# Score and softmax tiles turned over in 32x32 blocks by VectorE instead of by TensorE, in an attention-plus-feed-forward kernel with a hand-listed order

## The chip, the cores and the metric

The kernel runs on one NeuronCore of one Trainium2 chip. The metric is the device time of one execution in microseconds (us). Five engines work beside each other, each through its own queue in order: TensorE (PE in the rows, with its weight loads as PEld), VectorE (DVE), ScalarE (ACT), GpSimd (POOL) and SyncE (SP), which issues all the DMA transfers of this kernel.

## The reference

Two stages, all in fp32. First attention between 512 tokens and 32 state rows, per batch (8) and head (8, of width 64), in both directions; then a feed-forward layer with a rational activation over the 8 x (512 + 32) = 4352 rows that come out.

```python
scores = scale * x @ state.T                     # 512 x 32 per head
scores = scores - scores.max(-1)                 # over the 32 state rows
a = exp(scores); a /= a.sum(-1) + 1e-09
xread = a @ state
scores2 = scale * state @ x.T                    # 32 x 512 per head
scores2 = scores2 - scores2.max(-1)              # over the 512 tokens
a2 = exp(scores2); a2 /= a2.sum(-1) + 1e-09
sread = a2 @ x
x = concat([xread, sread])                       # rows x 512 columns
h = x @ w_in                                     # 512 -> 2048
P = a0 + a1*h + a2*h**2 + a3*h**3
Q = 1 + |b0|*|h| + |b1|*h**2
out = (P / (Q + 1e-6)) @ w_out                   # 2048 -> 512
```

## The kernel before, in words

**Work units.** The feed-forward is cut into 72 units: nine groups of eight. Group b below 8 is the 512 tokens of batch b, the ninth group holds all state rows. A unit n takes 256 of the 2048 hidden columns (u = n mod 8). The list name `F:n:i` is its first product (six matmuls of 128 x 512 for each of two column halves), `FC` and `FB` read the product h on ScalarE, `mu`, `po`, `qd`, `g1`, `g2`, `g3` are six VectorE instructions of 128 x 1024, `qa`, `ln`, `ex` three on ScalarE, and `gl` is one on GpSimd. `mh:n:t` and `ml:n:t` are the second product for token tile t (four and two matmuls of 128 x 512), which read the high and the low part of g (`gh`, `gl`). Products are taken with operands split in a rounded high part and a low rest, which is why one product of the reference is three here.

**Attention of a batch.** `scores` puts 32 x 256 products in PSUM so that a head pair's state row stands in a quadrant of 32 partitions and tokens run along the free axis. `sc_copy` (ScalarE, L414) copies them to SBUF as `sT`. The direction over tokens takes its maximum and its exponential from `sT` (`col_max`, `col_exp`). For the direction over the 32 state rows, `row_T` turns `sT` over: eight products of 128 x 128 with the identity (L434) into the PSUM tile `ps_s`; `row_max` (L458) and `row_sub` (L466) on VectorE read it, and `row_sub` writes the SBUF tile `e1`. Then `row_exp` (ScalarE), `row_sum`, `row_eps` (VectorE) and `row_norm` (GpSimd) follow, all on `e1`. `a_T` turns `e1` back with eight products (L434) into the PSUM tile `ps_a`; `a_hi` (ScalarE, L517) and `a_lo` (VectorE, L521) write its high and low part to `aT`, which the batch's eight `F` units read. `e2_T` is a third set of eight products. In the trace `e1` and `e2` are both called e.

**Weights.** The weights come as 64-bit floats in 32 pieces of 512 KB (`lr`). `cp` (ScalarE, L299), `jr` (VectorE, L309, two instructions per pair of pieces) and `jl` (VectorE, L325) make fp32 of them. For `w_out`, `sp` splits them (ScalarE L336, GpSimd L337). For `w_in`, `X` multiplies the state into the weights on TensorE (L606), `XA` copies the result out (ScalarE L618), `XS` stores it to DRAM, and `lm` and `fs` fetch it later for the units (L646, L647).

**Order.** `ORDER` is a list of 2266 such tokens. The program is emitted in that order, so the order of each engine's queue is the list's; the framework adds the waits. PSUM has two buffers of 128 x 1024 (tag h), shared by the units' h, `X`, and for batches 1 to 7 the tiles of `scores`, `row_T`, `e2_T`, `a_T` and `sread`. Four more banks hold the four running output tiles.

Of the kernel before, what the change touches and what calls it, by code (L numbers as in the profile page):

```python
# [18 lines left out]
P = 128  # L19
# [4 lines left out]
    "warm:8 lt:0:0 lr:0 cp:0 ls:0:2 scores:0:0 lr:1 jr:0 cp:1 jl:0 lc cb lt:0:1 scores:0:1 sc_copy:0:0 "  # L24
    "col_max:0:0 sc_copy:0:1 col_max:0:1 col_scale:0:0 lr:2 cp:2 X:0 fh:0 XA:0 col_scale:0:1 "
    "col_exp:0:1 lr:3 row_T:0:1 row_max:0:1 ls:2:8 row_sub:0:1 jw:0 XS:0 jr:1 X:3 fo:0 row_T:0:0 "
    "col_exp:0:0 X:1 row_exp:0:1 row_sum:0:1 lr:4 row_max:0:0 lr:5 XA:3 XS:3 cp:3 XA:1 row_sub:0:0 XS:1 "
    "e2_T:0:0 e2_copy:0:0 X:2 row_exp:0:0 lr:6 row_eps:0:1 row_norv:0:1 jl:1 a_T:0:1 row_sum:0:0 "
    "row_eps:0:0 a_hi:0:1 cp:4 XA:2 XS:2 e2_T:0:1 lr:7 X:5 row_norv:0:0 e2_copy:0:1 a_T:0:0 a_lo:0:1 "
    "col_eps:0 a_hi:0:0 a_lo:0:0 XA:5 XS:5 X:4 fh:1 cp:6 F:0:1 lq:0:0 fo:1 F:0:0 cp:5 jr:2 jl:2 b0a "  # L30
    "jr:3 XA:4 FC:0 lq:0:1 FB:0 qd:0 F:1:1 cp:7 F:1:0 lr:9 FB:1 FC:1 jl:3 XS:4 sp:7 sp:6 mu:0 po:0 qa:0 "
    "ln:0 qd:1 ex:0 jw:1 X:9 XA:9 lr:8 cp:8 lr:11 mu:1 po:1 lr:10 cp:10 XS:9 sread:0:0 cp:9 X:8 XA:8 "
    "XS:8 col_norm:0 jr:5 jr:4 jl:4 X:6 fh:2 fo:2 sread:0:1 sr_copy:0 g1:0 g2:0 XA:6 cp:11 lr:13 XS:6 "
    "qa:1 lr:15 sr_T:0 sr_fin:0 lr:14 jl:5 lr:12 g3:0 gl:0 X:12 fh:3 XA:12 XS:12 F:2:1 F:2:0 FC:2 FB:2 "
    "fo:3 sp:10 mh:0:0 mu:2 X:13 XA:13 XS:13 ln:1 sp:11 cp:12 qd:2 ex:1 mh:0:1 ml:0:1 cp:14 mh:0:2 "
    "ml:0:2 po:2 g1:1 g2:1 X:7 XA:7 jr:6 X:10 XA:10 ml:0:0 jr:7 cp:15 jl:7 lt:1:1 g3:1 gl:1 cp:13 qa:2 "
    "ln:2 X:11 XS:7 F:3:1 F:3:0 FB:3 FC:3 XA:11 jl:6 mh:0:3 ml:0:3 mh:1:3 ex:2 lt:1:0 scores:1:0 "
    "scores:1:1 XS:10 mu:3 qd:3 po:3 sp:14 sp:15 ml:1:3 lr:16 sc_copy:1 cp:16 lr:17 jw:4 mh:1:0 "
    "col_max:1 qa:3 lr:21 XS:11 X:17 X:14 XA:17 jw:2 jr:8 ml:1:0 g1:2 g2:2 g3:2 cp:17 ml:1:2 "
    "col_scale:1 XA:14 lr:20 X:15 XS:17 mh:1:2 row_T:1 row_max:1 row_sub:1 ln:3 mh:2:1 XS:14 jl:8 jw:3 "  # L40
    "cp:20 XA:15 XS:15 col_exp:1:0 cp:21 X:16 XA:16 lr:18 col_exp:1:1 gl:2 XS:16 lr:19 col_eps:1 fh:4 "
    "fo:4 X:18 XA:18 XS:18 row_exp:1 mh:1:1 cp:18 jr:10 jl:10 ml:1:1 X:20 fh:5 XA:20 fo:5 cp:19 F:4:1 "
    "F:4:0 FB:4 jr:9 col_norm:1 jl:9 X:21 FC:4 mh:2:2 mu:4 qd:4 sp:18 mh:2:3 XA:21 ml:2:1 sp:19 mh:2:0 "
    "lr:25 ex:3 ml:2:3 po:4 lr:22 XS:20 cp:22 g1:3 lr:23 cp:23 lr:24 cp:24 jr:12 XS:21 X:19 XA:19 XS:19 "
    "X:23 XA:23 cp:25 jr:11 jl:11 qa:4 lr:26 g2:3 g3:3 ml:2:0 sp:23 jl:12 X:22 sp:22 F:5:1 F:5:0 XS:23 "
    "FB:5 FC:5 mh:3:0 ml:2:2 mu:5 po:5 XA:22 cp:26 qd:5 lr:27 ln:4 mh:3:2 mh:3:1 XS:22 X:24 ex:4 g1:4 "
    "XA:24 XS:24 fh:6 fo:6 lm:8 mh:3:3 gl:3 lq:1:1 qa:5 ml:3:3 ml:3:0 X:26 XA:26 XS:26 ml:3:2 g2:4 g3:4 "
    "e2_T:1 e2_copy:1 row_sum:1 jr:13 cp:27 gl:4 X:25 XA:25 X:28 row_eps:1 row_norm:1:1 XS:25 jl:13 "
    "jw:7 mh:4:0 ln:5 ex:5 fh:7 F:6:1 XA:28 fo:7 g1:5 row_norm:1:0 F:6:0 FC:6 FB:6 qd:6 fs:8 ml:4:0 "
    "sp:26 ml:4:3 sp:27 XS:28 X:27 XA:27 lr:30 cp:30 ml:3:1 mu:6 po:6 qa:6 ln:6 ml:4:1 mh:4:2 lq:1:0 "  # L50
    "mh:4:3 X:30 XA:30 sread:1:0 sread:1:1 sr_copy:1 lr:28 g2:5 g3:5 gl:5 ex:6 mh:5:1 lr:31 mh:4:1 "
    "sr_T:1 sr_fin:1 cp:31 XS:27 XS:30 lr:29 X:29 XA:29 X:31 XA:31 mh:5:0 a_T:1 F:7:0 jr:15 F:7:1 jl:15 "
    "cp:28 ml:5:2 sp:31 mh:5:2 ml:5:3 g1:6 g2:6 a_hi:1 ml:4:2 a_lo:1 F:8:0 F:8:1 ml:5:1 sp:30 jr:14 "
    "cp:29 ml:5:0 FC:7 FB:7 mh:5:3 jl:14 qd:7 sp:29 sp:28 mh:6:3 mh:6:2 mu:7 po:7 mh:6:0 mh:6:1 lm:9 "
    "fs:9 FB:8 qd:8 qa:7 g3:6 F:9:1 F:9:0 gl:6 ml:6:2 ml:6:3 ln:7 ex:7 g1:7 mh:7:1 mh:7:2 FC:8 mu:8 "
    "po:8 FC:9 lm:10 ml:6:1 fs:10 FB:9 mh:7:3 F:10:1 g2:7 qa:8 ln:8 ex:8 F:10:0 g3:7 gl:7 ml:7:0 lm:11 "
    "ml:7:2 ml:7:1 qd:9 qa:9 ml:6:0 mu:9 po:9 FC:10 lm:13 lt:2:0 g1:8 FB:10 g2:8 g3:8 lt:2:1 scores:2:0 "
    "scores:2:1 mh:7:0 fl:7:2 gl:8 mu:10 po:10 qd:10 sc_copy:2 col_max:2 lq:2:1 ml:7:3 fl:7:3 mh:8:2 "
    "fl:7:1 fs:11 mh:8:3 mh:8:1 ml:8:1 ln:9 ml:8:3 ex:9 row_T:2 F:11:0 g1:9 g2:9 fl:7:0 mh:8:0 ml:8:0 "
# [872 lines left out]
```

## Time and profile before

| | us |
|---|---|
| median of 3 runs | 691.34 (690.94 to 692.08) |
| the profiled execution | 690.54 |
| its span, first to last instruction | 688.7 |
| TensorE busy | 661.9 (96%) |
| VectorE busy | 620.1 (90%) |
| ScalarE busy | 524.1 (76%) |
| GpSimd busy | 298.7 (43%) |
| mean granted TensorE clock | 0.987 of full speed |

The device time is 1.84 us longer than the span. Busy shares are means over the whole program; the program has a stage in which weights are fetched and converted, about 100 us long, a long middle in which one batch's units follow on another's, and an end of some 7 us.

### The profile page before, as it was taken

The page shows a single profiled execution, that of the slowest core. Times are in us where ns is not written, and L with a number is a line of the kernel's source. Part 1 is how long each engine was busy: PE and PEld are TensorE (multiplying, and loading weights), DVE is VectorE, ACT ScalarE, POOL GpSimd, SP SyncE. Part 2 cuts the span into 40 slices and gives each one's busy share as a digit, 9 for nine tenths or more (in the row PEclk, how much of TensorE's full clock was granted, in tenths as well). Part 3 has the DMA queues.
Part 4 walks back from the last instruction along what each step waited for, and adds up shares of the span by engine and source line. Part 5 has one row for each costly group of instructions (what it writes and reads, how often), then busy time and mean ns, then how long its engine had stood idle before and what let it go on. Part 6 is the DMA issues. An engine that isn't in the chain of part 4 may idle for free.

```text
span 688.7 us, 11564 instructions
## 1 busy us (share of the span) xinstructions
PE 661.9 (96%) x4602; PEld 525.3 (76%) x4602; DVE 620.1 (90%) x589; ACT 524.1 (76%) x641; POOL 298.7 (43%) x172
## 2 busy tenths in 40 slices
PE   6688889999999999999999999999999999999997
PEld 4455556778887778878887888788878788888895
DVE  4788689999999999999999999999899889998996
ACT  5889789887876876877778677777887777666773
POOL 0024146554554454434554444354444445445542
PEclk8989999999999999999999999999999999999999
DMA  7988877605122300451015022221203021300311
GB/s 290 327 298 327 304 290 277 225 37 196 64 77 92 127 17 25 125 190 39 18 60 199 15 98 72 92 82 71 78 33 137 2 75 55 99 0 33 107 47 30
DMA packets 29434, 81.49 MB, mean 118 GB/s; under 512 B 3268, under 2 KB 3396, under 8 KB 29380
## 3 DMA queue, kind: packets, MB, share of 16 engines
q1 hardware_dynamic: 29380, 80.75, 33.8%
q8 instruction: 36, 0.59, 0.4%
q14 instruction: 18, 0.15, 0.1%
HBM read 52.95 MB, written 27.79 MB: 117 GB/s over the span
## 4 chain that ended last, share of the span: by engine, by line
PE 77%; DVE 7%; DMA 6%; ACT 5%; issue 2%; POOL 1%; SPq 0%; POOLq 0%; ACTq 0%; DVEq 0%
PE h L687 25%; DMA m_dram<-xo 3%; DMA raw<-in_w_in_dram 2%; ACT xo L618 2%; PE o__3063 L760 2%; PE ps_x L606 2%; PE o__5992 L760 2%; PE o__3659 L760 2%; PE o__4266 L760 2%; PE o__3652 L760 2%; PE o__3604 L760 2%; PE o__5977 L760 2%; PE o__5430 L760 2%; PE o__3107 L760 2%; PE o__4244 L760 2%
## 5 line engine op out<-in xcount | busy, mean ns | idle before, releaser
L750 POOL TENSOR_TENSOR gl<-C,L 128x1024 fp32r<-128x1024 f32 (+1 forms) x71 | 168.9, 2379 | 271.1 <-DVE C L743 170.0
L687 PE MATMUL h<-aT,m 128*128 128x512 f32 x768 | 188.6, 392 | 0.8 <-ACT xo L618 0.8
L687 PEld LDWEIGHTS h<-aT,m 128*128 128x128 f32 x768 | 143.1, 188 | 33.1 <-ACT xo L618 2.9
L699 ACT ACTIVATE C<-h,cst 128x1024 f32<-128x1024 f32 (+1 forms) x72 | 83.1, 1156 | 40.9 <-PE h L687 33.3
L706 ACT ACTIVATE A<-h,cst 128x1024 f32<-128x1024 f32 (+1 forms) x72 | 76.9, 1068 | 47.1 <-PE h L687 41.7
L731 DVE SCALAR_TENSOR_TENSOR gh<-C,cst,L 128x1024 fp32r<-128x1024 f32 (+1 forms) x72 | 95.6, 1328 | 13.1 <-ACT L L802 9.5
L720 DVE SCALAR_TENSOR_TENSOR A<-A,b0a,h 128x1024 f32<-128x1024 f32 (+1 forms) x72 | 87.4, 1214 | 14.2 <-ACT A L706 10.4
L647 POOL TENSOR_TENSOR m<-m_sb,m 128x512 fp32r<-128x512 f32 x56 | 75.0, 1348 | 46.1 <-ACT m L646 22.0
L743 DVE SCALAR_TENSOR_TENSOR C<-C,cst,A 128x1024 f32<-128x1024 f32 (+1 forms) x72 | 91.0, 1263 | 2.1
L714 DVE SCALAR_TENSOR_TENSOR C<-C,cst,h 128x1024 f32<-128x1024 f32 (+1 forms) x72 | 87.7, 1219 | 1.9
L737 DVE SCALAR_TENSOR_TENSOR A<-A,gh 128x1024 f32<-128x1024 f32 (+1 forms) x72 | 87.5, 1216 | 1.7
L710 DVE TENSOR_TENSOR C<-C,h 128x1024 f32<-128x1024 f32 (+1 forms) x72 | 83.0, 1154 | 5.3 <-ACT C L699 2.7
L726 ACT ACTIVATE A<-A 128x1024 f32<-128x1024 f32 (+1 forms) x72 | 72.7, 1012 | 15.4 <-DVE A L720 15.4
L792 ACT ACTIVATE L<-A 128x1024 f32<-128x1024 f32 (+1 forms) x72 | 73.0, 1015 | 3.4 <-POOL gl L750 0.5
L802 ACT ACTIVATE L<-L 128x1024 f32<-128x1024 f32 (+1 forms) x72 | 73.1, 1015 | 1.8
L606 PE MATMUL ps_x<-win_sb,st 64*32 64x256 f32 x1024 | 39.6, 432 | 12.3 <-ACT xo L618 6.1
L337 POOL TENSOR_TENSOR wo<-cv_r,wo 128x512 fp32r<-128x512 f32 x16 | 23.3, 1476 | 59.8 <-ACT wo L336 59.6
L606 PEld LDWEIGHTS ps_x<-win_sb,st 64*32 64x32 f32 x1024 | 18.5, 116 | 28.1 <-issue 10.8
L646 ACT CAST m<-m_sb 128x512 fp32r<-128x512 f32 x56 | 33.9, 615 | 2.9 <-PE h L687 2.9
L618 ACT COPY xo<-ps_x 128x1024 f32<-128x1024 f32 (+1 forms) x32 | 28.8, 908 | 5.3 <-DMA m_dram<-xo 4.1
L299 ACT ACTIVATE cv_y<-raw 128x512 f32<-128x512 f32 x32 | 21.9, 695 | 11.1 <-DMA raw<-in_w_in_dram 8.7
L687 PEld LDWEIGHTS h<-sh,m 128*128 128x128 f32 x192 | 24.1, 191 | 0.6
(266 smaller groups left out, 1124.0 us busy)
## 6 DMA issues: line engine op xcount, KB each, us to landing
m_sb<-m_dram SPq DMA_DIRECT2D x56, 256.0 KB, 3.7
m_dram<-xo SPq DMA_DIRECT2D x24, 512.0 KB, 4.6
out_dram<-o_sb SPq DMA_DIRECT2D x34, 256.0 KB, 3.3
xT_sb<-in_xT_dram SPq DMA_DIRECT2D x16, 512.0 KB, 5.0
raw<-in_w_in_dram SPq DMA_DIRECT2D x16, 512.0 KB, 6.8
raw<-in_w_out_dram SPq DMA_DIRECT2D x16, 512.0 KB, 6.0
x_sb<-in_x_dram SPq DMA_DIRECT2D x16, 512.0 KB, 5.0
w_in_dram<-win_sb SPq DMA_DIRECT2D x8, 512.0 KB, 4.2
```

The lines of the kernel that those rows point to most:

```text
L647: nc.gpsimd.tensor_tensor(m[:, 1], t, m[:, 0].bitcast(F32), op=ALU.subtract)
L687: nc.tensor.matmul(h[:, ci * W : (ci + 1) * W], l, r, start=(q == 0), stop=(q == len(seq) - 1),)
L699: nc.scalar.activation(e["C"], e["h"], AF.Identity, scale=cst[:, 3:4], bias=cst[:, 2:3])
L706: nc.scalar.activation(e["A"], e["h"], AF.Abs, scale=cst[:, 5:6])
L710: nc.vector.tensor_tensor(e["C"], e["C"], e["h"], op=ALU.mult)
L714: nc.vector.scalar_tensor_tensor(e["C"], e["C"], cst[:, 1:2], e["h"], op0=ALU.add, op1=ALU.mult)
L720: nc.vector.scalar_tensor_tensor(e["A"], e["A"], b0a, e["h"], op0=ALU.add, op1=ALU.mult)
L731: nc.vector.scalar_tensor_tensor(e["gh"], e["C"], cst[:, 0:1], e["L"], op0=ALU.add, op1=ALU.mult)
L737: nc.vector.scalar_tensor_tensor(e["A"], e["A"], 1.0 + 1e-6, e["gh"].bitcast(F32), op0=ALU.add, op1=ALU.mult)
L743: nc.vector.scalar_tensor_tensor(e["C"], e["C"], cst[:, 0:1], e["A"], op0=ALU.add, op1=ALU.subtract)
L750: eng.tensor_tensor(e["gl"], e["C"], e["L"], op=ALU.mult)
L760: nc.tensor.matmul(O[t], e[l][:, j * W + t * P : j * W + (t + 1) * P], wo[:, k, 2 * u + j, :], start=(place == FIRST[n // U, t] and i + j ...
```

## The change

`row_T` and `a_T` become VectorE block transposes: one instruction that turns every 32 x 32 block over in its own place. Heads stand in quadrants of 32 partitions with 32 state rows each, so a block of tokens by state rows is such a block. `row_T` reads the PSUM tile of `scores` directly and writes `e1` in SBUF; `ps_s` and `ps_a` are gone. `row_max` and the subtraction now read `e1`. The subtraction is on GpSimd for all but the first half of batch 0 (`row_sup`). `a_T` writes a new SBUF tile `eT`, which for batches 1 to 7 has the buffer of `e2`; `a_hi` and `a_lo` read that, and `a_lo` is on GpSimd for batches 2, 3 and half of batch 0 (`a_lp`), on VectorE for the rest.

The list is ordered anew from its first token to its last, with 2266 tokens again. Beside the above it has other engines for some steps: 9 of the 32 copies `XA` are on VectorE (`XV`, four of 128 x 512 and five of 128 x 1024); 15 of the 16 pairs of `jr` are on GpSimd (`jp`); 3 of the 16 splits `sp` have their second half on VectorE (`sv`); one more `gl` and one more copy of an output tile are on VectorE (`gv`, `fv`). At the start SP issues the two halves of batch 0's `xT` and the first state rows before any weights. In the code:

```diff
@@ ORDER, first line @@
-    "warm:8 lt:0:0 lr:0 cp:0 ls:0:2 scores:0:0 lr:1 jr:0 cp:1 jl:0 lc cb lt:0:1 scores:0:1 sc_copy:0:0 "
+    "warm:8 lt:0:1 ls:0:2 lt:0:0 scores:0:0 scores:0:1 row_T:0:0 row_max:0:0 row_sub:0:0 lr:0 cp:0 "
...
@@ -329,12 +329,12 @@
     def store_win(u):
         nc.sync.dma_start(w_in32[u], win_t[u])
 
-    def conv_split(i):
+    def conv_split(i, eng):
         _, u, k = unit(i)
         m = CV[i // 2][1][:, k].bitcast(F32)
         f = 2 * u + k
         nc.scalar.copy(wo[:, 0, f, :], m)
-        nc.gpsimd.tensor_tensor(
+        eng.tensor_tensor(
             wo[:, 1, f, :], m, wo[:, 0, f, :].bitcast(F32), op=ALU.subtract
         )
 
@@ -365,6 +365,9 @@
                 for j in range(2)
             ]
         return ps_h.tile([P, 2, S], F32, name=name, tag="h")
+
+    def flat(t):
+        return t.rearrange("p j t -> p (j t)") if len(t.shape) == 3 else t
 
     def half(t, j):
         if isinstance(t, list):
@@ -438,7 +441,9 @@
                 )
 
     def row_T(b, j=None):
-        transposes(b, "ps_s", 2, TS[b]["sT"], j)
+        e1 = once(b, "e1", at_tile("e1", [P, 2, S]))
+        for i in (0, 1) if b == 0 and j is None else (j,):
+            nc.vector.transpose(flat(half(e1, i)), flat(half(TS[b]["ps"], i)))
 
     def col_exp(b, j):
         T = TS[b]
@@ -456,16 +461,16 @@
     def row_max(b, j=None):
         mx = once(b, "mx", at_tile("mx", [P, NT * 8], 2))
         nc.vector.tensor_reduce(
-            stat(mx, j), slots(TS[b]["ps_s"], j), axis=AX.X, op=ALU.max
-        )
-
-    def row_sub(b, j=None):
+            stat(mx, j), slots(TS[b]["e1"], j), axis=AX.X, op=ALU.max
+        )
+
+    def row_sub(b, j=None, eng=None):
         T = TS[b]
-        e1 = once(b, "e1", at_tile("e1", [P, 2, S]))
+        e1 = slots(T["e1"], j)
         mx = stat(T["mx"], j)
-        nc.vector.tensor_tensor(
-            slots(e1, j),
-            slots(T["ps_s"], j),
+        (eng or nc.vector).tensor_tensor(
+            e1,
+            e1,
             mx.unsqueeze(2).broadcast_to([P, mx.shape[1], NS]),
             op=ALU.subtract,
         )
@@ -509,18 +514,19 @@
         )
 
     def a_T(b, j=None):
-        transposes(b, "ps_a", 2, TS[b]["e1"], j)
-
-    def a_hi(b, j=None):
+        t = once(b, "eT", lambda: at.tile([P, 2, S], F32, name="eT", tag="e2" if b else "e2T"))
+        nc.vector.transpose(flat(half(t, j)), flat(half(TS[b]["e1"], j)))
+
+    def a_hi(b, j=None, copy=None):
         if b not in AT:
             AT[b] = at.tile([P, 2, 2, S], F32R, name="aT", tag="aT", bufs=2)
-        nc.scalar.copy(half(AT[b][:, 0], j), half(TS[b]["ps_a"], j))
-
-    def a_lo(b, j=None):
+        (copy or nc.scalar.copy)(half(AT[b][:, 0], j), half(TS[b]["eT"], j))
+
+    def a_lo(b, j=None, eng=None):
         a = AT[b]
-        nc.vector.tensor_tensor(
+        (eng or nc.vector).tensor_tensor(
             half(a[:, 1], j),
-            half(TS[b]["ps_a"], j),
+            half(TS[b]["eT"], j),
             half(a[:, 0].bitcast(F32), j),
             op=ALU.subtract,
         )
@@ -821,7 +827,8 @@
         "jr": lambda k: join_rest(k, nc.vector),
         "jp": lambda k: join_rest(k, nc.gpsimd),
         "jl": join_low,
-        "sp": conv_split,
+        "sp": lambda i: conv_split(i, nc.gpsimd),
+        "sv": lambda i: conv_split(i, nc.vector),
         "fh": fold_hi0,
         "fo": fold_lo0,
         "fs": fold_split,
@@ -861,6 +868,8 @@
         "fd": store,
         "lc": load_const,
         "cb": spread_const,
+        "a_lp": lambda b, j=None: a_lo(b, j, nc.gpsimd),
+        "row_sup": lambda b, j=None: row_sub(b, j, nc.gpsimd),
         "row_norv": lambda b, j: row_norm(b, j, nc.vector),
         "b0a": lambda: nc.scalar.activation(b0a, cst[:, 4:5], AF.Abs),
     }
```

TensorE's queue around the scores of batch 5 (`ps_s` is the transposed scores, `o` the running output tiles, `h` a unit's first product). Before:

```order
L760 MATMUL o__3659<-wo,gl 128x512 x2
L760 MATMUL o__3604<-wo,gl 128x512 x2
L434 MATMUL ps_s<-ident,sT 128x128 x8
L760 MATMUL o__3652<-wo,gh 128x512 x4
L687 MATMUL h<-aT,m 128x512 x18
L760 MATMUL o__3604<-wo,gl 128x512 x4
```

and now, from the batch's scores (`ps_sc`) on:

```order
L407 MATMUL ps_sc<-xT_sb,st 32x256 x16
L766 MATMUL o__3559<-wo,gl 128x512 x2
L766 MATMUL o__3564<-wo,gh 128x512 x4
L766 MATMUL o__3607<-wo,gh 128x512 x4
L766 MATMUL o__3607<-wo,gl 128x512 x2
L766 MATMUL o__3616<-wo,gh 128x512 x4
```

The eight products into `ps_s` have gone out of the queue, and nothing stands in their place but the second products that were around them.

VectorE's queue at the same place (`mx` is the row maximum, `cm` the column maximum, `e_3739` and `e_3667` are e1 of batch 5). Before:

```order
L418 TENSOR_REDUCE cm<-sT 128x2
L720 SCALAR_TENSOR_TENSOR A<-A,b0a,h 128x1024
L428 TENSOR_SCALAR cm<-cm 128x2
L743 SCALAR_TENSOR_TENSOR C<-C,cst,A 128x1024
L458 TENSOR_REDUCE mx<-ps_s 128x32
L466 TENSOR_TENSOR e_3739<-ps_s,mx 128x1024
L731 SCALAR_TENSOR_TENSOR gh<-C,cst,L 128x1024
```

and now:

```order
L421 TENSOR_REDUCE cm<-sT 128x2
L726 SCALAR_TENSOR_TENSOR A<-A,b0a,h 128x1024
L737 SCALAR_TENSOR_TENSOR gh<-C,cst,L 128x1024
L743 SCALAR_TENSOR_TENSOR A<-A,gh 128x1024
L431 TENSOR_SCALAR cm<-cm 128x2
L749 SCALAR_TENSOR_TENSOR C<-C,cst,A 128x1024
L446 STREAM_TRANSPOSE e_3667<-ps_sc 128x1024
L463 TENSOR_REDUCE mx<-e_3667 128x32
L737 SCALAR_TENSOR_TENSOR gh<-C,cst,L 128x1024
```

The transpose has come in ahead of the row maximum, and the subtraction behind it has left for GpSimd's queue; a second transpose (`eT`) stands 25 instructions further on.

GpSimd's queue at the start of the program (`wo` the low part of `w_out`, `cv_r` the joined weight bits). Before, from its first piece of work on:

```order
L337 TENSOR_TENSOR wo<-cv_r,wo 128x512 x2
L750 TENSOR_TENSOR gl<-C,L 128x1024
L337 TENSOR_TENSOR wo<-cv_r,wo 128x512 x2
L750 TENSOR_TENSOR gl<-C,L 128x1024
L337 TENSOR_TENSOR wo<-cv_r,wo 128x512 x2
```

and now:

```order
L309 TENSOR_SCALAR cv_r<-raw 128x512 x4
L512 TENSOR_TENSOR e_127<-e_127,rs 128x512
L471 TENSOR_TENSOR e_127<-e_127,mx 128x512
L309 TENSOR_SCALAR cv_r<-raw 128x512 x2
L527 TENSOR_TENSOR aT<-eT,aT 128x512
L309 TENSOR_SCALAR cv_r<-raw 128x512 x2
L337 TENSOR_TENSOR wo<-cv_r,wo 128x512 x2
L309 TENSOR_SCALAR cv_r<-raw 128x512 x4
L756 TENSOR_TENSOR gl<-C,L 128x1024
```

Joins of weight bits and batch 0's softmax steps now stand ahead of the first split and the first `gl`.

## Rows read from the trace of the kernel before

**Rows 1.** The page's span, and the busy time of each engine (us, share of the span, instructions).

```profile
span 688.7 us, 11564 instructions
PE 661.9 (96%) x4602; PEld 525.3 (76%) x4602; DVE 620.1 (90%) x589; ACT 524.1 (76%) x641; POOL 298.7 (43%) x172
```

**Rows 2.** Busy time of each engine in five stretches of the span: from and to in us, length, then busy us and instructions of PE, PEld, DVE, ACT and POOL, the granted TensorE clock, the share of the DMA engines and GB/s.

```profile
0.00:100.00 100.00, 79.73 (x1091) 50.41 (x1092) 73.57 (x99) 77.81 (x113) 20.12 (x18) 0.91 0.84 305
100.00:140.00 40.00, 39.75 (x456) 28.38 (x455) 38.56 (x35) 36.69 (x48) 25.50 (x15) 1.00 0.72 258
140.00:620.00 480.00, 478.16 (x2688) 390.16 (x2687) 450.96 (x389) 366.63 (x422) 223.08 (x122) 1.00 0.23 77
620.00:682.00 62.00, 62.00 (x365) 55.13 (x365) 55.73 (x68) 42.38 (x59) 30.00 (x18) 1.00 0.16 52
682.00:688.70 6.70, 2.25 (x9) 1.22 (x7) 1.27 (x2) 0.59 (x1) 0.00 (x0) 0.96 0.26 78
```

**Rows 3.** Waits of TensorE from 100 us on: who waited for whom, us in total, times, longest.

```profile
PE o__4923 L760 <- POOL gl L750: 1.0, 1, 1.0
PE o__2418 L760 <- POOL gl L750: 0.5, 1, 0.5
PE o__1819 L760 <- POOL gl L750: 0.4, 1, 0.4
PE ps_sr L539 <- DVE C L714: 0.2, 1, 0.2
```

**Rows 4.** The two sets of products with the identity that the change touches, batches 1 to 7 (duration ns min/median/max, first and last start in us), and the timeline of TensorE around one set, batch 7's (start us, us, what).

```profile
L434 PE MATMUL ps_s<-ident,sT x56: 270/272/273, 72.6 to 510.4; 128*128 128x128 f32 x56
L434 PE MATMUL ps_a<-ident,e x56: 270/272/273, 127.3 to 549.7; 128*128 128x128 f32 x56
...
509.62 1.04 PE L434 MATMUL ps_s<-ident,sT 128*128 128x128 f32 x8
510.42 1.17 PE L760 MATMUL o__4244<-wo,gh 128*128 128x512 f32 x4
```

**Rows 5.** Groups of VectorE instructions from 100 to 682 us (busy us, mean ns of one | idle before).

```profile
L521 DVE TENSOR_TENSOR aT<-ps_a,aT 128x1024 fp32r<-128x1024 f32 x7 | 8.5, 1217 | 1.4 <-ACT aT L517 1.4
...
L466 DVE TENSOR_TENSOR e<-ps_s,mx 128x1024 f32<-128x1024 f32 x6 | 7.3, 1224 | 0.2
L458 DVE TENSOR_REDUCE mx<-ps_s 128x32 f32<-128x1024 f32 x6 | 7.3, 1217 | 1.0 <-PE ps_s L434 1.0
...
L657 DVE TENSOR_TENSOR m<-win_sb,m 128x512 fp32r<-128x512 f32 x8 | 7.1, 903 | 0.3 <-issue 0.2
...
L309 DVE TENSOR_SCALAR cv_r<-raw 128x512 int32<-128x512 uint32 x6 | 5.8, 1014 | 0.0
...
L750 DVE TENSOR_TENSOR gl<-C,L 128x512 fp32r<-128x512 f32 x1 | 0.7, 693 | 0.1
```

**Rows 6.** Groups of GpSimd instructions from 100 to 682 us, same columns.

```profile
L750 POOL TENSOR_TENSOR gl<-C,L 128x1024 fp32r<-128x1024 f32 x61 | 151.8, 2489 | 227.4 <-DVE C L743 135.2 <-PE h L687 20.2 <-ACT m L646 10.5
L647 POOL TENSOR_TENSOR m<-m_sb,m 128x512 fp32r<-128x512 f32 x56 | 75.0, 1348 | 46.1 <-ACT m L646 22.0 <-issue 16.6 <-DVE gh L731 3.9
...
L810 POOL TENSOR_TENSOR sh<-srT,sh 128x1024 fp32r<-128x1024 f32 x1 | 2.4, 2411 | 0.0
```

**Rows 7.** The three VectorE steps with two inputs in SBUF from 100 to 682 us (groups), one of them over the whole program (ns min/median/max), and the longest one beside GpSimd's instruction of that moment (timeline).

```profile
L731 DVE SCALAR_TENSOR_TENSOR gh<-C,cst,L 128x1024 fp32r<-128x1024 f32 x60 | 84.1, 1402 | 10.1 <-ACT L L802 7.2 <-PE o__5447 L760 1.2 <-PE o__2423 L760 0.7
L743 DVE SCALAR_TENSOR_TENSOR C<-C,cst,A 128x1024 f32<-128x1024 f32 x60 | 78.6, 1309 | 1.8
L737 DVE SCALAR_TENSOR_TENSOR A<-A,gh 128x1024 f32<-128x1024 f32 x60 | 77.1, 1285 | 1.3
...
L731 DVE SCALAR_TENSOR_TENSOR gh<-C,cst,L x72: 742/1280/3502, 43.8 to 679.5; 128x1024 fp32r<-128x1024 f32 x64, 128x512 fp32r<-128x512 f32 x8
...
209.08 3.50 DVE L731 SCALAR_TENSOR_TENSOR gh<-C,cst,L 128x1024 fp32r<-128x1024 f32 x1
...
209.11 2.39 POOL L750 TENSOR_TENSOR gl<-C,L 128x1024 fp32r<-128x1024 f32 x1 [1.81 <-PE o__1814 L760]
```

**Rows 8.** The longest waits of VectorE from 100 us on, the first two of 15 (us in total, times, longest).

```profile
DVE A L720 <- ACT A L706: 8.9, 13, 1.2
DVE gh L731 <- ACT L L802: 8.0, 12, 1.5
```

**Rows 9.** The first 100 us: waits of TensorE for ScalarE's copies `xo`, then groups of ScalarE (the copies) and VectorE (the joins).

```profile
PE ps_x L606 <- ACT xo L618: 6.1, 4, 2.7
...
PE ps_sc L404 <- ACT xo L618: 0.9, 1, 0.9
PE h L687 <- ACT xo L618: 0.8, 1, 0.8
...
L618 ACT COPY xo<-ps_x 128x1024 f32<-128x1024 f32 x17 | 17.0, 1013 | 3.7 <-DMA m_dram<-xo 3.3 <-PE ps_x L606 0.4
L618 ACT COPY xo<-ps_x 128x512 f32<-128x512 f32 x6 | 3.6, 594 | 0.9 <-ACT cv_y L299 0.9
...
L309 DVE TENSOR_SCALAR cv_r<-raw 128x512 int32<-128x512 uint32 x26 | 9.7, 424 | 9.0 <-DMA raw<-in_w_in_dram 7.8 <-DMA raw<-in_w_out_dram 1.2
```

**Rows 10.** A VectorE reduction over 128 x 512 (ns min/median/max) and a VectorE copy of 128 x 512 out of PSUM (timeline).

```profile
L458 DVE TENSOR_REDUCE mx<-ps_s__183 x1: 680/680/680, 16.8 to 16.8; 128x16 f32<-128x512 f32 x1
...
683.40 0.69 DVE L776 COPY o_sb<-o__5992 128x512 f32<-128x512 f32 x1 [0.82 <-PE o__5992 L760]
```

324 rows, old and new, of the table ORDER are left out of this document.

## The prediction

> **What bounds the kernel now.** I read the page's busy shares first: TensorE is busy 96% of the span, VectorE 90% [rows 1]. Shares over the whole span mix stages, so I cut the span into five stretches. In the first 100 us TensorE has 20.3 us idle and every engine some; from 100 to 682 us it is busy 579.9 of 582 us at the full granted clock; the last 6.7 us are the end [rows 2]. The list of waits says what those missing 2.1 us were: four, three of them for GpSimd's `gl`, the last for VectorE [rows 3]. So over 85% of the span TensorE's own work sets the time, and an instruction taken from it there is worth its full spacing, as long as nobody else becomes late. The engine that could is VectorE: 545.3 of the 582 us busy (38.6 + 451.0 + 55.7), that is 93.7%, with 36.7 us of holes [rows 2]. ScalarE (445.7) and GpSimd (278.6) have room there.
>
> **TensorE: what goes.** The removed products come as 8 per set, one set for `ps_s` and one for `ps_a` per batch. Each lasts 272 ns, but they overlap, so what counts is the spacing: in the timeline a set starts at 509.62 and the next product at 510.42, 0.80 us for 8 [rows 4]. The `ps_s` sets of batches 1 to 7 run from 72.6 to 510.4 us, so six fall behind 100 us; the `ps_a` sets run from 127.3 to 549.7, so all seven do [rows 4]. 13 x 0.80 = 10.4 us leave TensorE where it has no holes. Batch 0's sets and one of batch 1's lie in the first 100 us, where TensorE has 20.3 us idle beside them; I cost those at nothing, and if that cover were not there they would be worth some 2 us more.
>
> **VectorE: what comes and goes, 100 to 682 us.** A 32x32 transpose by VectorE is in no row. From below: the joins of weight bits take 424 ns for 128x512 when nothing disturbs them [rows 9], so 0.85 for 128x1024. From above: GpSimd's two-input step over the same shape, 2.41 [rows 6]. VectorE's other passes over 128x1024 fp32 take 1.217 (`mx`, one input) and 1.224 (`e`) whatever they compute [rows 5]; I take 1.22. Then: 13 transposes, +15.9. Six subtractions leave for GpSimd, -7.3. Two `a_lo` (batches 2 and 3) leave, -2.4. Three halves of weight splits come, at 903 ns for the alike `m` with both inputs in SBUF, +2.7. Six joins of 1014 ns leave (the disturbed ones), -5.8 [rows 5]. Two of the nine copies `XV` fall behind 100 us in the list, from 0.69 for 128x512 doubled less a fixed part, 1.2 each, +2.4 [rows 10]. One `gl` and one output copy of 0.69, +1.4 [rows 5, 10]. Sum +6.9.
>
> **GpSimd and what it does to VectorE.** GpSimd gains in this stretch six subtractions and two `a_lo` at 2.41, six joins, and loses three splits and a half-size `gl`; at 1.35 for a 128x512 step (the `m` row) +15.2 + 1.35 x (6 - 4) = 22 of 303 idle us: it fits [rows 2, 6]. But it is not free for VectorE. The three unit steps with two SBUF inputs have means of 1402, 1309 and 1285 ns where the undisturbed ones are about 1280, 1285 and 1224, and the worst, 3.50 us, starts with a `gl` that runs 2.39 [rows 7]. Over 60 of each that is 7.3 + 1.4 + 3.7 = 12.4 us for 278.6 us of GpSimd work, 4.5%; 22 us more cost VectorE 1.0. The rule behind it is in the Trainium skill, "SBUF — State Buffer", section "Who interferes with whom": a VectorE step with two SBUF inputs and a GpSimd step that reads SBUF exclude each other for a whole instruction. By this rule a VectorE `a_lo`, which read PSUM and SBUF and now reads SBUF twice, can stand behind a whole GpSimd step, at worst 2.41 us for each of five, 12 us; the trace agrees on the mechanism but not on the size. By the mean of the `gh` row it is 122 ns each, 0.6 us, too little to enter the sum. VectorE then needs 545.3 + 6.9 + 1.0 = 553.2 us.
>
> **Does that still fit?** TensorE's stretch becomes 582 - 10.4 = 571.6 us, so VectorE is at 96.8% and its holes are 18.4 us, half of 36.7. Its longest waits are for ScalarE's reads of h, 8.9 and 8.0 us [rows 8]; these are places where it was early, and being early less often is what fills them. What is queued behind a late VectorE step is the next unit's `gh`, for which `mh` on TensorE waits. TensorE's own waits were 2.1 us at 36.7 us of holes; letting them grow as the holes shrink gives 2.1 x 36.7 / 18.4 = 4.2, so +2.1 us. Below, they stay as they are (0); above, see the rivals. `row_sub` on GpSimd and `row_norm` stand in one queue with `gl`; a batch's `a_T` on VectorE waits for them, with the six steps of the units behind it, which TensorE's queue of other units' products covers as long as the list places it late enough.
>
> **The first 100 us.** TensorE waits 7.8 us for ScalarE's copies `xo` there (6.1 + 0.9 + 0.8) [rows 9]. Nine of the 32 copies go to VectorE, four halves of 0.594 and five of 1.013: ScalarE has 7.4 us less. VectorE loses 26 joins of 424 ns (11.0, less the one pair it keeps) and gets seven copies, about 6.4, and batch 0's transposes. GpSimd, busy 20.1 of 100 us [rows 2], takes the joins: its 128x512 steps take 1.35, so 1.9 us more per pair than on VectorE, at the head of the chain from raw weights to `X`. The batch's first products get their inputs earlier by one transfer's place in SP's queue. From below all 7.8 us of waits go; from above the joins are late throughout and it loses as much. I take 2 us gained, since ScalarE, the busiest of the three with 77.8, is relieved and GpSimd has room.
>
> **Sum.** 688.7 - 10.4 - 2.0 + 2.1 = 678.4 us span. The execution lay 1.84 above its span, 680.2; the median of the runs lies 0.8 above this profiled execution: 681.0 us.
>
> **Rivals.**
> 1. *VectorE becomes the bound and the kernel slower.* If its holes do not shrink, because each is a chain through ScalarE and not earliness, the stretch takes 553.2 + 36.7 = 589.9: span 98 + 589.9 + 6.7 = 694.6, time 697. It decides from the point where more than 30.8 us of holes stay (98 + 553.2 + 30.8 + 6.7 = 688.7). For it: the two long waits name ScalarE [rows 8]. Against: TensorE loses only 2.1 us today, so most holes cost nothing. 8%.
> 2. *The transpose is dear.* At 2.41 us, 13 x 1.19 = 15.5 more: VectorE needs 568.7, with half its holes (18.4) 587.1, span 691.8, time 694. From about 2.2 us on it turns slower. Against it: every VectorE pass of this shape in the rows takes 1.2 to 1.3 undisturbed [rows 5, 7]. The Trainium skill, "VectorE: DVE Perf Modes", section "The three transpose paths", gives 311 ns for a 128x128 block on VectorE. Eight of these, an estimate from that page, are 2.5 us and would be this rival; but 128 columns carry the fixed part, and the rows' 680 and 1217 ns for 512 and 1024 columns [rows 5, 10] leave 0.14 fixed and 0.28 for 128 columns, close to the page's figure. 4%.
> 3. *The start gets longer.* If GpSimd's joins (2.41 instead of 1.35) or the new order hold `X` back by 8 us instead of gaining 2: 691. For: 30 steps of unknown price at the head of a chain. 6%.
> 4. *VectorE paces part of the way.* With two thirds of its holes left (24.5), 98 + 553.2 + 24.5 + 6.7 = 682.4, time 685. 12%.
> 5. *Better.* All waits for `xo` go and no new ones come: 688.7 - 10.4 - 7.8 = 670.5, time 673. For: two PSUM tiles per batch less compete for the two h buffers. 11%.
>
> **How the numbers follow.** Forecast 59%, its own range 677 to 685. The range 674 to 691 holds it, rival 4, half of 3 and half of 5; left out are 1, 2 and the other halves, 20%. What a measurement here tells from no change is about 0.2%, 1.4 us. Faster by more: forecast, 4, 5 and a third of 3, 84%; within it: 3%; slower: 1, 2 and the rest, 13%.
>
> **What would show it.** Right: from 100 us on TensorE still above 99% busy, VectorE at 96 to 98%, the transpose rows near 1.2 us, the waits of TensorE there at 3 to 6 us, TensorE's busy time some 12 us less. Wrong: transposes of 2 us; many waits of TensorE on `gh` or h behind VectorE; `a_lo` or `gh` rows with means well above 1.4; or a first stretch whose TensorE idle time is far from 18 us.

## The result, and the profile after

The changed kernel takes 695.81 us (five runs, 694.46 to 696.59), the kernel before 690.94 beside it. The ratio is 1.0072, with a 95% interval of 1.0049 to 1.0096: slower by 0.7%, where 681.0 had been forecast. The profiled execution took 696.03 us, its span 694.3.

The page's span and busy times of the changed kernel, in the columns of [rows 1]:

```profile
span 694.3 us, 11328 instructions
PE 649.2 (94%) x4474; PEld 513.9 (74%) x4474; DVE 626.5 (90%) x580; ACT 516.3 (74%) x631; POOL 383.9 (55%) x209
```

TensorE does what was promised of it: 128 products fewer and 12.7 us less busy (661.9 before). Yet the span is 5.6 us longer, so its idle time rose by 18.3, from 26.8 to 45.1 us. The cut into stretches, with the columns of [rows 2], says where:

```profile
0.00:100.00 100.00, 66.32 (x953) 41.52 (x961) 68.60 (x76) 65.83 (x94) 68.44 (x40) 0.88 0.82 290
100.00:140.00 40.00, 36.56 (x481) 24.57 (x466) 32.55 (x32) 30.27 (x42) 34.65 (x18) 0.91 0.65 230
140.00:620.00 480.00, 476.71 (x2658) 387.10 (x2657) 463.55 (x400) 374.58 (x435) 251.44 (x135) 1.00 0.24 81
620.00:687.00 67.00, 67.00 (x387) 59.20 (x386) 60.10 (x73) 45.01 (x62) 29.33 (x19) 1.00 0.19 60
687.00:694.30 7.30, 2.62 (x11) 1.52 (x9) 1.67 (x3) 0.59 (x1) 0.00 (x0) 1.00 0.24 72
```

In the first 140 us TensorE is idle for 37.1 us (33.68 + 3.44) where it was 20.5 [rows 2]: 16.6 of the 18.3. Some 3 us of these are only the place of the four sets of products of batches 0 and 1 that are gone there (an estimate, 4 x 0.80 us by [rows 4]). From 140 us to the end of the middle it is idle 3.3 us, against 1.8. GpSimd's busy time in the first 100 us went from 20.1 to 68.4, while TensorE, VectorE and ScalarE all do less there than before. TensorE's waits of the first 140 us, as in [rows 3], the first four:

```profile
PE ps_x L612 <- DVE m L641: 7.9, 2, 6.5
PE ps_x L612 <- DVE A L726: 6.3, 2, 5.7
PE ps_x L612 <- DVE win_sb L325: 6.2, 2, 5.3
PE o__600 L766 <- POOL gl L756: 3.4, 1, 3.4
```

The row that names ScalarE's copies, 6.1 us before [rows 9], has shrunk to 2.6; in its place `X` waits for VectorE, which is itself only 69% busy. So VectorE waits for somebody, and its own first two waits of the same stretch say for whom (the joins are `cv_r`, the joined piece of `w_in` is `win_sb`):

```profile
DVE win_sb L325 <- POOL cv_r L309: 9.5, 4, 3.9
DVE cv_r L325 <- POOL cv_r L309: 9.1, 4, 2.6
```

The chain of waits shows one such place step by step (start, us, what; the lengths are those of the pieces that the chain goes through, so `win_sb`, which runs 1.23 us, has 0.04 here):

```profile
40.53 1.96 POOL cv_r L309
...
42.56 2.00 POOL cv_r L309
...
44.62 3.00 POOL cv_r L309
...
47.70 1.96 POOL cv_r L309
...
49.69 0.04 DVE win_sb L325
...
50.83 0.70 DVE m L641
...
51.57 1.96 PE ps_x L612 x32
```

Four joins run 9.1 us in a row. VectorE's `win_sb` stands behind them, `m`, which empties a PSUM tile for the next `X`, stands behind that in VectorE's queue, and `X` waits 6.5 us for `m`: the last link, not the late one. A wait's row names who came last; who was late is found by asking the named engine for its own waits. The group of the joins, then their durations (ns min/median/max, first and last start):

```profile
L309 POOL TENSOR_SCALAR cv_r<-raw 128x512 int32<-128x512 uint32 x30 | 70.3, 2343 | 10.6 <-DMA raw<-in_w_in_dram 8.4
...
L309 POOL TENSOR_SCALAR cv_r<-raw x30: 1945/1998/3007, 9.0 to 144.6; 128x512 int32<-128x512 uint32 x30
...
L309 DVE TENSOR_SCALAR cv_r<-raw x2: 419/419/419, 70.1 to 70.4; 128x512 int32<-128x512 uint32 x2
```

The one pair that stayed on VectorE takes 419 ns per step. GpSimd takes 1998 (median) for the same step.

The middle does most of what the prediction said. Groups of 140 to 687 us, in the columns of [rows 5] and [rows 7], and the waits of TensorE from 145 us on:

```profile
L446 DVE STREAM_TRANSPOSE e<-ps_sc 128x1024 f32<-128x1024 f32 x6 | 7.5, 1243 | 0.0
L518 DVE STREAM_TRANSPOSE eT<-e 128x1024 f32<-128x1024 f32 x6 | 7.4, 1240 | 0.0
...
L527 DVE TENSOR_TENSOR aT<-eT,aT 128x1024 fp32r<-128x1024 f32 x5 | 6.1, 1214 | 0.0
...
L737 DVE SCALAR_TENSOR_TENSOR gh<-C,cst,L 128x1024 fp32r<-128x1024 f32 x58 | 84.7, 1462 | 5.8 <-ACT L L808 2.6 <-PE o__5344 L766 1.1 <-PE o__4815 L766 0.5
...
L471 POOL TENSOR_TENSOR e<-e,mx 128x1024 f32<-128x1024 f32 x6 | 13.5, 2250 | 0.0
```

```profile
PE o__2941 L766 <- DVE gh L737: 1.4, 1, 1.4
PE o__1790 L766 <- POOL gl L756: 0.8, 1, 0.8
PE o__4747 L766 <- DVE gh L737: 0.6, 1, 0.6
PE o__5877 L766 <- DVE gl L756: 0.2, 1, 0.2
```

A block transpose takes 1.24 us, out of PSUM or out of SBUF. VectorE is at 96.6% from 140 to 620 us (463.55 of 480) and at 95.7% from 140 to 687 us (523.65 of 547); TensorE waits 3.0 us in all.

### The profile page after: what moved, and what is told of

Read it like the earlier page. It is cut to its first block, busy times and chain, and to the rows that moved or that the text cites. A ratio compares the mean times of both kernels' runs of the same rounds, so it can differ in the third digit from the quotient of the medians.

```text
span 694.3 us, 11328 instructions
## 1 busy us (share of the span) xinstructions
PE 649.2 (94%) x4474; PEld 513.9 (74%) x4474; DVE 626.5 (90%) x580; ACT 516.3 (74%) x631; POOL 383.9 (55%) x209
## 4 chain that ended last, share of the span: by engine, by line
PE 74%; POOL 9%; DVE 8%; issue 3%; ACT 3%; DMA 2%; SPq 0%; DVEq 0%; POOLq 0%; ACTq 0%
PE h L693 24%; POOL cv_r L309 6%; DVE gh L737 2%; PE o__2398 L766 2%; PE o__5372 L766 2%; PE o__3607 L766 2%; PE o__4206 L766 2%; PE o__3559 L766 2%; PE o__2389 L766 2%; PE o__4132 L766 2%; PE o__5302 L766 2%; PE o__4786 L766 2%; PE o__4138 L766 2%; PE o__3012 L766 2%; PE o__2366 L766 2%
## 5 line engine op out<-in xcount | busy, mean ns | idle before, releaser
L737 DVE SCALAR_TENSOR_TENSOR gh<-C,cst,L 128x1024 fp32r<-128x1024 f32 (+1 forms) x72 | 99.9, 1389 | 10.9 <-ACT L L808 4.4
L749 DVE SCALAR_TENSOR_TENSOR C<-C,cst,A 128x1024 f32<-128x1024 f32 (+1 forms) x72 | 88.6, 1232 | 2.2
L309 POOL TENSOR_SCALAR cv_r<-raw 128x512 int32<-128x512 uint32 x30 | 70.3, 2343 | 10.6 <-DMA raw<-in_w_in_dram 8.4
L624 ACT COPY xo<-ps_x 128x1024 f32<-128x1024 f32 (+1 forms) x23 | 21.5, 939 | 11.1 <-PE ps_x L612 7.2
```

What stands on the lines that cost most here:

```text
L309: eng.tensor_scalar(CV[k][1][:, j], RAW[2 * k + j][:, :, 0], 2.0**-29, 7.0, op0=ALU.mult, op1=ALU.min,)
L737: nc.vector.scalar_tensor_tensor(e["gh"], e["C"], cst[:, 0:1], e["L"], op0=ALU.add, op1=ALU.mult)
L749: nc.vector.scalar_tensor_tensor(e["C"], e["C"], cst[:, 0:1], e["A"], op0=ALU.add, op1=ALU.subtract)
```

## The experiments

Theory J: the joins on GpSimd delay the chain raw weights, join, `win_sb`, `X`, and so cost the start more than the middle gains. Rivals: theory O, the new order of the start or the copies given to VectorE, and theory V, VectorE and its block transposes in the long middle. Times are medians. The ratio is that to the kernel before, measured beside each run, with its 95% interval; the runs are from several chips, so where medians and ratios lead to different readings, both are given.

**The joins alone, from both sides.** In the changed list the joins go back to VectorE; in the list of before they go to GpSimd.

```diff
@@ ORDER of the changed kernel, 15 tokens @@
-jp:k
+jr:k
```

> The changed kernel, its list untouched, with the 15 pairs of joins that it has on GpSimd put back on VectorE; nothing else differs. Theory J (the joins: each takes 2.0 us on GpSimd, where it took 0.42 on VectorE, at the head of the chain from raw weights to X, and this is what the first 140 us lose): TensorE's idle time in the first 140 us falls from 37 us to about 20, and the time to 676 to 684 us. Theory O (the new order of the list or the copies XV on VectorE lose it): TensorE's idle time there stays above 30 us and the time above 690. Theory V (VectorE in the long middle is what binds): TensorE's idle time from 140 us on grows, and the time stays above 690 too.

Measured: 685.45 us, ratio 0.9901 (0.9867 to 0.9936), 10.4 us less than the changed kernel (11.8 by the ratios). That is J's sign, but the time lies just above J's band. The span's two parts, in the profiled executions: TensorE's idle time falls from 45.1 to 39.5, its busy time from 649.2 to 644.8 for the same 4474 products, with the granted clock over the span at 0.994 instead of 0.978. So 5.6 us are waits that are gone, and 4.4 are the same products running shorter at the higher clock; in a second execution of this kernel (last experiment: 38.2 idle, 646.3 busy, 0.992) it is 6.9 and 2.9. But in the first 140 us TensorE is still idle for 32.1 us (28.26 + 3.84), where J had expected about 20:

```profile
0.00:100.00 100.00, 71.74 (x1056) 45.22 (x1057) 80.92 (x103) 72.42 (x103) 24.79 (x21) 0.97 0.87 313
100.00:140.00 40.00, 36.16 (x436) 25.25 (x435) 38.10 (x41) 30.98 (x42) 15.05 (x10) 1.00 0.69 236
140.00:620.00 480.00, 477.15 (x2634) 388.38 (x2633) 462.66 (x401) 375.74 (x434) 248.99 (x134) 1.00 0.23 77
```

The joins cost some 10 us, and TensorE's waits in the new beginning have other causes beside them.

```diff
@@ ORDER of the kernel before, 16 tokens @@
-jr:k
+jp:k
```

> The kernel before, its list untouched, with all 16 pairs of joins on GpSimd. Theory J: its first 140 us lengthen by about as much as the changed kernel's did, 8 to 18 us, so 699 to 709 us. Theory O: the joins alone do little, within 3 us of the kernel before (688 to 694).

Measured: 718.86 us, ratio 1.0381 (1.0341 to 1.042): 28 us, far above the band. The sign is J's, the size is not. A likely reason, not tried by itself, is that the list of before has the joins closer to their reader `jl`, 8.6 tokens on average against 13.7 in the changed list. VectorE waits 51.2 us for them in eight places:

```profile
L306 POOL TENSOR_SCALAR cv_r<-raw x32: 1938/1956/2994, 5.9 to 160.2; 128x512 int32<-128x512 uint32 x32
...
who waited for it (us, times):
  DVE cv_r L322: 27.8, 5
  DVE win_sb L322: 23.4, 3
```

**Only the head of the chain.** The changed kernel with the first five pairs on VectorE and the other ten on GpSimd.

```diff
@@ ORDER of the changed kernel, k = 0 to 4 @@
-jp:k
+jr:k
```

> The changed kernel with the first five of its 15 pairs of joins on GpSimd put back on VectorE, ten stay. If the delay at the head of the chain is what costs: 7 us or more of e1's 10.4 come back (685 to 689 us). If it is GpSimd's load over the whole start (15 pairs, about 4.7 us each): a third of it, 3 to 4 us (691 to 693).

Measured: 688.21 us, ratio 0.9971 (0.9949 to 0.9994). The first 100 us:

```profile
0.00:100.00 100.00, 74.14 (x1057) 46.25 (x1058) 79.73 (x92) 72.77 (x105) 53.83 (x34) 0.95 0.89 317
```

Five of fifteen pairs bring 7.6 of the 10.4 us, though GpSimd is still busy 53.8 of the first 100 us (24.8 with all joins back). At 3.2 us more per pair, the first five are 16 us longer on GpSimd and cost 7.6, the other ten are 32 us longer and cost 2.8. So it is mostly the length of the steps at the head that costs, and not the load of GpSimd.

**The block transposes alone.** The list and the engines of before, with the new `row_T` and `a_T`; subtraction and `a_lo` stay on VectorE, and `eT` has the buffer of `sT` (in the trace VectorE never sits idle before `eT`).

```diff
     def row_T(b, j=None):
-        transposes(b, "ps_s", 2, TS[b]["sT"], j)
+        e1 = once(b, "e1", at_tile("e1", [P, 2, S]))
...
+            nc.vector.transpose(flat(half(e1, i)), flat(half(TS[b]["ps"], i)))
...
```

> The kernel before, its list and its engines, with the block transposes of VectorE alone: the subtraction and a_lo stay on VectorE, all joins stay on VectorE, eT has sT's buffer. If the removed products are worth their spacing (13 x 0.80 us) and VectorE's two more passes per batch (2 x 1.24 us) fit in its holes: 680 to 686 us, with TensorE's waits from 140 us on at 3 to 6 us. If VectorE binds in a list that was not made for it: TensorE's waits there above 10 us and 689 us or more.

Measured: 706.52 us, ratio 1.0202 (1.0158 to 1.0246), 15.9 us slower than before. The stretch from 140 to 620 us, and TensorE's longest wait there:

```profile
140.00:620.00 480.00, 461.07 (x2525) 365.39 (x2526) 461.00 (x392) 357.23 (x414) 226.00 (x120) 1.00 0.23 78
...
PE h L690 <- DVE aT L524: 2.2, 2, 1.7
```

VectorE has no larger share here (96.0%) than in the changed kernel (96.6%), yet TensorE is idle for 18.9 us instead of 3.3, in many small waits for `gh`, `gl`, `aT` and `sr`. One of the late steps is `a_lo`: in that stretch it took 1.71 us on average here and 1.21 in the changed kernel, and its longest took 3.40, starting at 352.58 beside a `gl` of GpSimd that started at 351.54 and took 3.36. In the old list the same load on VectorE falls where TensorE needs it; the new list and the steps given to GpSimd together make room, and no run parts the two.

**The subtraction.** The changed kernel with its joins back, and the subtractions on VectorE too.

```diff
@@ ORDER of the changed kernel with jr @@
-row_sup:b
+row_sub:b
```

> e1_joins_back with the eight subtractions back on VectorE too (seven of them 128x1024 at 1.22 us). VectorE is 96.4% busy from 140 to 620 us in e1. If it is the second bound there, as e3 suggests (18.9 us of TensorE idle in that stretch): TensorE's idle time there grows from 2.9 to 6 us or more and the time by 4 to 9 us. If VectorE's holes still cover it: within 2 us of e1 (685.5).

Measured: 691.11 us, ratio 1.0014 (0.9986 to 1.0043), 5.7 more than with the joins back alone. From 140 to 620 us TensorE is idle 5.8 us, just short of the 6 expected, instead of 2.9 (474.17 and 477.15 busy):

```profile
140.00:620.00 480.00, 474.17 (x2606) 383.72 (x2605) 462.72 (x402) 370.41 (x428) 233.66 (x126) 1.00 0.23 76
```

So the offload is worth some 3 us there; the rest lies in the first 140 us, where the granted clock of the first 100 was 0.90 instead of 0.97, and stays unexplained.

**The copies.** The joins back, and all copies `xo` back on ScalarE.

```diff
@@ ORDER of the changed kernel with jr, 9 tokens @@
-XV:u
+XA:u
```

> As e1_joins_back, and the nine copies XV back on ScalarE as well. Theory J: the copies weigh little beside the joins, within 3 us of e1 on either side. Theory O with the copies as its cause: several us faster than e1, and e1 itself above 690.

Measured: 696.07 us, ratio 1.0066 (1.004 to 1.0092): 10.6 us worse, a miss for both sides. TensorE's waits of the first 140 us for copies, first the longest here, then all with nine copies on VectorE (joins back in both):

```profile
PE h L690 <- ACT xo L621: 6.1, 4, 2.9
...
PE ps_x L609 <- DVE xo L621: 1.9, 1, 1.9
PE ps_x L609 <- ACT xo L621: 1.3, 2, 1.0
PE h L690 <- DVE xo L621: 1.1, 2, 0.8
PE h L690 <- ACT xo L621: 0.9, 2, 0.6
```

With the copies back, the waits for ScalarE's are 6.9 us in all, about as long as before the change (7.8). So giving the copies to VectorE was a gain, and the prediction's reason for it shows; but it took only 4.7 us of these waits away and brought 3.0 of waits for VectorE's copies, so most of the 10.6 us stays unexplained.

**The old beginning with the new middle.** The list of before, with its engines and its products for batches 0 and 1, up to a seam; from there the tokens of the changed list that are still missing, in its order and with its engines but the joins on VectorE. The seam lies behind `F:8:1` in the one and behind `scores:2:1` in the other.

```diff
     def row_T(b, j=None):
+        if b < 2:
+            transposes(b, "ps_s", 2, TS[b]["sT"], j)
+            return
         e1 = once(b, "e1", at_tile("e1", [P, 2, S]))
...
```

> The list of the kernel before up to F:8:1 (its first 136 us, with its engines and with products with the identity for batches 0 and 1), then the rest of the changed kernel's list with its engines, joins on VectorE; batches 2 to 7 use block transposes. If the changed kernel's middle is sound and only its start is at fault: TensorE loses 6 sets of ps_s and 6 of ps_a, 12 x 0.80 = 9.6 us, gains about 1 us of waits, and the start stays as before: 680 to 684 us, below e1_joins_back. If the middle's gain hangs on the start that its list was made with (the units in flight at the seam do not fit): waits of TensorE from 140 us on above 8 us and 687 or more.

Measured: 683.6 us, ratio 0.9912 (0.9894 to 0.993), inside the band of a sound middle.

> As e5, with the seam later, behind batch 2's scores (about 155 us). Same theories; both seams alike (within 2 us of each other) says that the seam itself costs little.

Measured: 680.6 us, ratio 0.9887 (0.9847 to 0.9928), 9.35 us below before by the medians and 7.8 by the ratio, and below both kernels. The two seams lie 3.0 us apart, more than the 2 expected, so the seam's place may count for something; the four runs reach from 679.42 to 685.02. Its stretches:

```profile
0.00:100.00 100.00, 78.82 (x1095) 51.00 (x1096) 74.79 (x99) 78.97 (x114) 21.20 (x19) 0.97 0.86 309
100.00:140.00 40.00, 39.11 (x454) 27.96 (x453) 38.30 (x35) 36.38 (x47) 23.74 (x14) 1.00 0.73 253
140.00:620.00 480.00, 477.43 (x2645) 388.71 (x2644) 461.39 (x401) 372.17 (x430) 250.27 (x133) 1.00 0.23 76
```

TensorE is idle 22.1 us in the first 140 and 2.6 in the middle. Twelve sets of products are gone here, 9.6 us at 0.80 each: the middle's gain is there as soon as the beginning costs nothing.

**The weights' place in SyncE's queue.** With the joins back, 4.8 us remain between the medians of the new beginning (685.45) and the old (680.6). By the ratios, 0.9901 and 0.9887, it is 1.0 us, and their intervals overlap, so this remainder is not clear of noise. One suspect is that the new list loads batch 0's tokens ahead of the first weights.

```diff
-    "warm:8 lt:0:1 ls:0:2 lt:0:0 scores:0:0 scores:0:1 row_T:0:0 row_max:0:0 row_sub:0:0 lr:0 cp:0 "
+    "warm:8 lt:0:1 lr:0 ls:0:2 lr:1 lt:0:0 scores:0:0 scores:0:1 row_T:0:0 row_max:0:0 row_sub:0:0 cp:0 "
...
```

> The changed list with its joins back on VectorE, and SyncE's first loads in the order of before (the first two pieces of weights behind the first half of batch 0's tokens, and not behind both halves and the state rows); nothing else is moved. With the joins back the changed list took 685.45, the old beginning with the new middle 680.6. If the old beginning is 4.8 us better because its weights arrive earlier, this kernel takes 681 to 683, and the wait of TensorE's X for win_sb in the first 100 us (5.9 us in three waits with the joins back) shrinks below 4. If the difference comes from batch 0's softmax steps and the copies that stand among the joins in VectorE's queue, it takes 685 to 686.

> The changed kernel with its joins back on VectorE once more, beside the run with the weights first on the same chip: 684 to 687 by every theory.

Measured: 687.61 us with the weights first, ratio 0.9951 (0.9933 to 0.9968), and 685.04 without, ratio 0.9907 (0.9883 to 0.9931). The suspect falls: with the weights first the time is 2.6 us longer, above the ranges of both theories, the wait for `win_sb` shrank by only 1.0 us (6.1 to 5.1), and batch 0's scores waited 4.4 us for tokens instead of 2.4. The repeat agrees with the first measurement within 0.4 us.

## Why the prediction was wrong

**Right: the middle.** "13 x 0.80 = 10.4 us leave TensorE where it has no holes": with the old beginning, twelve sets less, 9.6 us by that price, gave 7.8 to 9.35 us. TensorE's busy time fell by 12.7, which is 16 sets of 0.80 over the whole program, but so close a match is in part luck, since the clock moves that time too (15.6 to 17.1 less with the joins back). The transposes cost 1.24 us where 1.22 was taken, so the dear transpose is out. The 311 ns that this rival took from the Trainium skill, "VectorE: DVE Perf Modes", section "The three transpose paths", are given there for bf16; the tiles here are fp32. VectorE at 96.8% was forecast for all that follows the first 100 us; from 140 to 687 us it was 95.7%. TensorE's waits from 145 us on were 3.0 us, where the forecast let 2.1 grow to 4.2. The worst case that was weighed for `a_lo`, each behind a whole GpSimd step, did not come in this list (1214 ns, 1217 before); it came once in the old list, with 3.40 us. With the old beginning this middle gives 680.6 us; 681.0 had been forecast, though with 2.0 us from the start in it. One figure in the recorded sum for GpSimd is a slip: eight steps at 2.41 us are 19.3, not 15.2, and the 22 is right.

**Wrong: the term "The first 100 us".** Its words were that GpSimd's steps "take 1.35, so 1.9 us more per pair than on VectorE, at the head of the chain from raw weights to `X`", and then "I take 2 us gained, since ScalarE, the busiest of the three with 77.8, is relieved and GpSimd has room". Two faults lie in it. The size: a join takes 1.998 us, not 1.35, so a pair costs 2 x (1.998 - 0.419) = 3.2 us more. And the reasoning: the price was set against GpSimd's free time, though the prediction itself says that the joins head a chain. Engine room hides a step only if nobody waits for it. Instead of gaining 2 us, the new beginning cost some 15 us beside the old one with the same middle (695.81 against 680.6; 12.8 by the ratios), of which the joins are 10.4 (11.8). The prediction's own sign came: TensorE's idle time in the first stretch was 33.7 us, far from 18. The bound "from above the joins are late throughout and it loses as much" was an arbitrary mirror: the four joins in the chain above took 9.1 us in a row, and four at 0.42 would have taken 1.7.

**The rival that came.** It is the third, "The start gets longer", with 6%. It named the cause, as one of two, and was itself too small: 691 at 2.41 us per join, 695.8 measured at 1.998. Its 8 us of delay were a guess, not a sum along the chain.

**Not seen by any case.** Three things. The longer idle times at the start go with a lower granted clock, and the same products took 2.9 to 4.4 us longer, a part of the 10.4 us that the joins cost. The new beginning shows no gain over the old one even without GpSimd's joins. And the rival in which VectorE becomes the bound was argued from the number of its holes, while the run of the block transposes in the old list shows that it depends on where its steps stand and what they are: it came there at the same busy share.

**Open.** Whether the new beginning, with the joins back, really is slower than the old one (4.4 to 4.8 us by the medians, 1.0 to 1.4 by the ratios, not clear of noise), and by what. It is not the weights' place, and not the copies on VectorE. Left are batch 0's softmax steps between the joins in VectorE's queue, and the block transposes of batches 0 and 1 themselves, which were products on TensorE in both runs with the old beginning. With the joins back most of TensorE's waits there still name VectorE, but neither was tried by itself.

## What to carry to other kernels

Before a step moves to an engine with room, ask whether somebody waits for its result: at the head of a chain much of a step's added length can reach the end (here 7.6 of 16 us for the first five pairs, 2.8 of 32 for the rest), and the engine's share does not tell it. Judge a change stage by stage, and undo it stage by stage: here a middle worth 8 to 9 us was hidden by a beginning that lost more. And a busy share of 96% on the second engine left TensorE idle 3.3 us in one arrangement and 18.9 in another, so its load and its list must be changed together.

## What the hardware showed that was not expected

**The clock falls with the gaps.** In the changed kernel TensorE's `X`, 32 products each, go out after gaps of different length. Stretches around three of them, in the columns of [rows 2]:

```profile
33.10:38.80 5.70, 0.01 (x1) 0.00 (x0) 5.66 (x7) 4.35 (x6) 1.27 (x1) 0.75 1.03 420
38.80:40.80 2.00, 1.96 (x32) 0.76 (x32) 2.00 (x2) 2.00 (x4) 1.56 (x2) 0.50 1.02 410
44.00:45.10 1.10, 1.10 (x40) 0.49 (x32) 0.52 (x1) 1.10 (x3) 1.02 (x2) 1.00 1.13 242
45.10:51.50 6.40, 0.02 (x3) 0.00 (x0) 2.52 (x4) 3.63 (x4) 4.47 (x2) 0.85 0.54 187
51.50:53.40 1.90, 1.83 (x32) 0.68 (x32) 1.90 (x3) 0.00 (x0) 0.00 (x0) 0.50 0.00 0
```

Behind idle stretches of 5.7 and 6.4 us the clock is at its lower level, 1.2 GHz (0.50), and 32 products take 1.96 us in the timeline; in between, at 2.4 GHz (1.00) and behind other products, the same ones take 1.09. So each of these two waits cost 0.87 us more after it had ended.

**A join is dear on GpSimd.** It reads only one input, and takes 4.8 times as long as on VectorE (1998 against 419 ns); the two-input fp32 step that had served as its price took 1.35 us [rows 6]. Whether the integer types or the step over every second word makes it so was not tried.

**The lock works both ways.** The join of 44.62 us, which started beside a VectorE step with two inputs in SBUF, took 3.00 us where its neighbours took 1.96 to 2.00. The other way round is the `a_lo` of 3.40 us above, beside a step of GpSimd. The VectorE step beside the join:

```profile
44.58 1.23 DVE L325 SCALAR_TENSOR_TENSOR cv_r<-cv_y,cv_r 128x1024 int32<-128x1024 int32 x1 [2.36 <-POOL cv_r L309]
```

The Trainium skill says in "SBUF — State Buffer", section "Who interferes with whom", that such a VectorE step and GpSimd's reads shut each other out for an instruction; the 1.04 us agree with it.
